# A sketched attention with a Fourier mix on one core: k alone in strided columns, last v tokens loaded apart, spare matmuls in a gap, and a new timetable of grouped matmuls

## The chip, the cores and the metric

One core of one Trainium2 chip. The metric is the time of one execution on the device in microseconds. Each kernel was run several times, and one execution was taken with the profiler. The profiled span runs from the first to the last instruction and is shorter than the time: in the runs told here by 1.8 to 2.5 us in nearly all of them, and by up to 3.4 us in a few.

With one core, a run counts as slow when it is over 1.5% above the fastest of the same kernel, and as fast otherwise. Ratios between kernels use fast runs alone, run on the same chip in the same rounds.

The engines are named as in the profile: PE is TensorE's matmuls and PEld its weight loads, DVE is VectorE, ACT is ScalarE, POOL is GpSimd, SP issues most transfers.

## The reference

Four batches of four heads, 1088 tokens, head size 32. The attention maps q and k to 64 products of two 8-wide projections each, and needs no softmax. Its output, 128 wide, goes through a Fourier transform over tokens and channels, of which the real part is kept, a normalization, and a two-layer filter. It is shown cut to what matters.

```python
def phi(x):                                   # x: (4, 4, 1088, 32)
    a = einsum('rd,bhsd->bhsr', S1, x)        # r = 8
    b = einsum('rd,bhsd->bhsr', S2, x)
    return einsum('bhsi,bhsj->bhsij', a, b).reshape(..., 64)
q_p, k_p = phi(q), phi(k)
kv = einsum('bhsf,bhsd->bhfd', k_p, v)
z = sum(k_p, axis=2)
x = einsum('bhsf,bhfd->bhsd', q_p, kv) / (einsum('bhsf,bhf->bhs', q_p, z)[..., None] + 1e-6)
x = x.transpose(0, 2, 1, 3).reshape(4, 1088, 128)
u = x + real(fft(fft(x, axis=1), axis=2))
un = (u - mean(u)) / sqrt(var(u) + 1e-6)
out = u + relu(un @ w_ch1) @ w_ch2            # (4, 1088, 128) float32
```

## The kernel before

The kernel first only notes its operations, each with one or more engines that could do it. Three lists then decide everything: `_SEQ` is the order in which the operations are issued, `_PICK` the engine of each, `_BANK` the PSUM bank of each product. Each engine works its own instructions in that order.

```python
def order(self, table):
    seq, picks, slots = table
    for o, x in zip(self.ops, picks):
        o.pick = x
    for bk, x in zip(self.banks, slots):
        bk.slot = x
    return [self.ops[n] for n in seq]
# ...
pe([(0.05, 0.2)] * WARM, e, ["dumw"], [bw], key=("prep", 0, "warm"), writes=["warm"], t=-15)  # 21 matmuls on zeros
```

A batch goes through this chain: load k, q and v; transpose k and q in blocks of 32x32 on DVE; project k, multiply the two halves (`kp`); k-times-v on PE, which needs v in `vx`; copy the result to `kvz`; project q in two large products, one of which is copied to `bsb`, mostly by ScalarE; multiply (`qp`); qp-times-kv; divide to the attention output `xb`. The mix of the batch follows: sums `yf` and `fo`, the transform (`zt`, `us`), the normalization, the two layers (`hT`), and the result `ob`, which is stored.

Buffers come in two sets, so batch 2's loads wait for batch 0's use. Loads stand in one queue in order. k and q are both transposed into strided columns:

```python
for i in range(3):                                                  # k: step of 4 fp32
    d = [[1, 2], [128, 8], [4, 32]]
    eng.transpose(_v(kT(s), 0, 128, 2 * i, d), kin(s)[:, 512 * i : 512 * i + 512])
    # ...
for i in range(3):                                                  # q: step of 8 fp32
    if STRIDED and i < 2:
        d = ([[1, 8], [256, 2], [8, 32]], [[-1, 8], [-256, 2], [8, 32]])[i]
        eng.transpose(_v(qT(s), 0, 128, o + (256 + 7) * i, d), qin(s)[:, o : o + 512])
```

v is loaded in four transfers of 288 columns; the tokens left over come in a fifth transfer that waits for those four, and the ninth and last group of k-times-v waits for it:

```python
for j in range(4):
    n = 288
    def e(q_, j=j, n=n):
        q_.dma_start(_v(vx(s), 0, 128, 640 * j, [[1, n]]), bass.AP(tensor=v.tensor, ...))
    inline(P.add(sp(128, 4 * n, e, [("vone", s)] + gate), key=("ld", b, "vx"), writes=[w], war=war, t=t))
# ...
P.add(sp(128, 128, e, [w]), aq(128, 128, e, [w]), key=("ld", b, "vr"), writes=[wr], war=war, t=t + 0.01)
# ...
pe(f32ct(64), e, [(("kp", c), b), ("vx", b), ("vone", s)] + ([("vr", b)] if c == 8 else []),
   [bkv], key=K("pkv", c), writes=[("pkv", b)], t=T + 4 + 0.5 * c, mode=1)
```

## Time and profile before

| | before |
|---|---|
| time, three runs | 90.91 us median, 90.26 to 91.88 |
| the profiled execution | 89.34 us, span 87.2 us, mean granted TensorE clock 0.98 |
| busy | PE 73.8, DVE 74.6, ACT 47.2, POOL 43.1 us |

This is PE's timeline of the kernel before, the rows that begin with a wait of over 0.3 us; columns are start and length in us, engine, line, operation, output and inputs, shapes, count, and in brackets the idle time before and what ended it:

```profile
1.22 4.44 PE L375 MATMUL bank<-dumw 128*128 128x256 bf16 x21 [1.22 <-DVE dumw L338]
8.40 1.95 PE L532 MATMUL bank<-sblk,kT 128*64 128x64 f32 x36 [2.74 <-DVE kT L500]
18.30 1.27 PE L532 MATMUL bank<-sblk,kT 128*64 128x64 f32 x36 [1.68 <-DVE kT L503]
34.47 0.27 PE L567 MATMUL bank<-vx,kp 128*64 128x64 f32 x1 [0.34 <-issue]
35.24 0.34 PE L532 MATMUL bank<-sblk,kT 128*64 128x64 f32 x4 [0.50 <-DVE kT L500]
38.85 0.23 PE L795 MATMUL bank<-cd,zt 128*128 128x128 bf16 x1 [0.45 <-ACT zt L281]
69.82 0.42 PE L753 MATMUL bank<-tab,fo 128*128 128x288 bf16 x2 [0.36 <-DVE fo L739]
```

The k projections (L532) of batches 0, 1 and 3 wait for k's transposition, in the head for 2.74 us. The same 36 matmuls take 1.95 us in the head and 1.27 us for batch 1: after the first gap the clock is halved.

### The profile page before, as it was taken

What the parts mean: (1) busy time and instruction counts of PE and PEld (TensorE: products, weight loads), DVE (VectorE), ACT (ScalarE), POOL (GpSimd) and SP (SyncE); (2) the same over time, 40 slices, a digit from 0 to 9 for tenths busy, and PEclk for the clock granted to TensorE, in tenths of its full rate; (3) what the DMA queues carried; (4) which work ended last, traced back from release to release, by engine and by line L of the source; (5) the groups of instructions that cost most, each with busy time, mean ns of one, the idle gap of its engine ahead of it and who ended that gap; (6) DMA issues with size and microseconds to landing.
All of it is one profiled execution on the core that took longest, in us unless ns stands there. A gap on an engine that the chain in (4) does not pass through costs nothing.

```text
span 87.2 us, 3358 instructions
## 1 busy us (share of the span) xinstructions
PE 73.8 (85%) x1348; PEld 55.2 (63%) x1351; DVE 74.6 (86%) x237; ACT 47.2 (54%) x129; POOL 43.1 (49%) x83
## 2 busy tenths in 40 slices
PE   4951999669999997879999999999899889998600
PEld 3731944554599956758896765796388656875500
DVE  1156979999999968999989999997999999999940
ACT  3500335015332227197999998724613999999300
POOL 7830398009949899489723220002992684620000
PEclk9999579999999999999999999999999999999999
DMA  0799999895006988000000000017260000002653
GB/s 0 167 288 346 391 368 355 315 417 224 1 8 169 297 326 271 19 8 4 8 0 0 0 23 0 0 25 209 64 213 0 4 0 8 0 0 68 190 147 106
DMA packets 8150, 10.98 MB, mean 126 GB/s; under 512 B 1608, under 2 KB 6728, under 8 KB 8136
## 3 DMA queue, kind: packets, MB, share of 16 engines
q1 hardware_dynamic: 6774, 9.80, 34.3%
q10 hardware_dynamic: 1362, 0.98, 4.0%
q8 instruction: 10, 0.16, 0.7%
q14 instruction: 4, 0.03, 0.1%
HBM read 8.55 MB, written 2.23 MB: 124 GB/s over the span
## 4 chain that ended last, share of the span: by engine, by line
PE 43%; DVE 33%; DMA 11%; ACT 3%; SPq 2%; issue 2%; DVEq 0%; ACTq 0%
DMA kin<-in_k_dram 11%; DVE qp L669 8%; PE bank L913 7%; PE bank L626 7%; DVE ob L933 6%; DVE kT L500 6%; PE bank L875 6%; PE bank L532 5%; PE bank L567 4%; DVE qT L519 3%; PE bank L795 3%; PE bank L753 3%; PE bank L692 3%; DVE xb L710 3%; PE bank L638 2%
## 5 line engine op out<-in xcount | busy, mean ns | idle before, releaser
L550 POOL TENSOR_TENSOR kp<-ab 128x256 f32<-128x256 f32 x23 | 13.7, 625 | 9.8 <-ACT ab L281 9.7
L883 ACT ACTIVATE hT<-bank 128x512 bf16<-128x512 f32 x25 | 13.6, 608 | 1.0 <-PE bank L875 1.0
L669 DVE TENSOR_TENSOR qp<-bank,bsb 128x512 f32<-128x512 f32 (+1 forms) x24 | 12.0, 541 | 0.5 <-ACT bsb L281 0.5
L567 PEld LDWEIGHTS bank<-vx,kp 128*64 128x64 f32 x288 | 9.9, 138 | 3.8 <-POOL kp L550 1.6
L729 POOL TENSOR_TENSOR yf<-xb 128x512 f32<-128x512 bf16 x6 | 6.9, 1157 | 10.6 <-DVE xb L710 10.6
L913 PE MATMUL bank<-w2b,hT 128*128 128x128 bf16 x144 | 11.9, 220 | 0.3 <-ACT hT L883 0.3
L567 PE MATMUL bank<-vx,kp 128*64 128x64 f32 x288 | 11.4, 224 | 0.3 <-issue 0.3
L739 POOL TENSOR_TENSOR fo<-yf 128x256 bf16<-128x256 f32 x15 | 11.1, 760 | 1.0 <-DVE yf L729 0.7
L913 PEld LDWEIGHTS <-hT 128*128 128x128 bf16 x144 | 9.0, 98 | 3.8 <-issue 1.0
L281 ACT COPY bsb<-bank 128x512 f32<-128x512 f32 (+1 forms) x21 | 8.2, 462 | 5.8 <-PE bank L626 5.0
L532 PE MATMUL bank<-sblk,kT 128*64 128x64 f32 x144 | 7.0, 242 | 5.1 <-DVE kT L500 3.2
L692 PE MATMUL bank<-kvz,qp 128*64 128x66 f32 x288 | 11.0, 225 | 0.3 <-DVE qp L669 0.3
L933 DVE SCALAR_TENSOR_TENSOR ob<-bank,rs,us 128x128 f32<-128x128 f32 (+1 forms) x36 | 10.2, 331 | 0.8 <-PE bank L913 0.7
L692 PEld LDWEIGHTS bank<-kvz,qp 128*64 128x64 f32 x288 | 10.0, 137 | 1.2 <-DVE qp L669 0.8
L281 ACT COPY ab<-bank 128x256 f32<-128x256 f32 (+1 forms) x7 | 2.8, 395 | 12.7 <-PE bank L532 10.1
L532 PEld LDWEIGHTS bank<-sblk,kT 128*64 128x64 f32 x144 | 5.9, 153 | 5.9 <-DVE kT L500 3.7
L875 PE MATMUL bank<-uT,w1c 128*128 128x512 bf16 x29 | 9.4, 379 | 0.2
L500 DVE STREAM_TRANSPOSE kT<-kin 128x512 f32<-128x512 f32 x8 | 8.2, 1090 | 1.2 <-DMA kin<-in_k_dram 1.2
L830 DVE BATCH_NORM_STATS2 st<-bank 128x6 f32<-128x128 f32 (+1 forms) x36 | 8.6, 272 | 0.2 <-PE bank L806 0.2
L519 DVE STREAM_TRANSPOSE qT<-qin 128x512 f32<-128x512 f32 x8 | 8.5, 1096 | 0.0
L281 ACT CAST zt<-bank 128x288 bf16<-128x288 f32 x16 | 6.1, 411 | 4.2 <-PE bank L753 4.1
L283 POOL CAST ub<-us 128x512 bf16<-128x512 f32 (+1 forms) x9 | 4.5, 506 | 5.8 <-ACT us L281 4.3
(82 smaller groups left out, 148.7 us busy)
## 6 DMA issues: line engine op xcount, KB each, us to landing
vx<-in_v_dram SPq DMA_DIRECT2D x16, 144.0 KB, 4.9
qin<-in_q_dram SPq DMA_DIRECT2D x4, 544.0 KB, 5.6
kin<-in_k_dram SPq DMA_DIRECT2D x3, 544.0 KB, 5.0
out_dram<-ob SPq DMA_DIRECT2D x9, 128.0 KB, 2.6
out_dram<-ob ACTq DMA_DIRECT2D x7, 128.0 KB, 2.4
tab<-tab_d SPq DMA_DIRECT2D x1, 864.0 KB
kin<-in_k_dram SPq DMA_DIRECT2D x1, 288.0 KB
kin<-in_k_dram SPq DMA_DIRECT2D x1, 256.0 KB, 3.2
```

Of the source, the lines that this page charges most:

```text
L281: SE.copy(o, i)
L500: eng.transpose(_v(kT(s), 0, 128, (2 if STRIDED else 64) * i, d), kin(s)[:, 512 * i : 512 * i + 512])
L519: eng.transpose(_v(qT(s), 0, 128, o + (256 + 7) * i, d), qin(s)[:, o : o + 512])
L532: PE.matmul(_v(bt(bks[bi]), 64 * th, 64, 64 * ci, [[1, 64]]), kT(s)[:, 128 * c + 64 * th : 128 * c + 64 * th + 64], sblk[:, :], start=True ...
L550: eng.tensor_tensor(out=_v(kp(s, c), 0, 128, 0, [[64, NH], [8, 8], [1, 8]]), in0=_v(bt(bks[i]) if eng is VE else ab(s, i), 0, 128, 64 * ci ...
L567: PE.matmul(_v(bt(bkv), 64 * hh, 64, 128 * p + 64 * hh, [[1, 64]]), _v(kp(s, c), 0, n, 128 * p + 64 * hh, [[1, 64]]), _v(vx(s), 0, 128, 32 ...
L669: P.add(dve(nd, lambda e, p=p, i=i, nd=nd, dd=dd, bA=bA, ah=ah: e.tensor_tensor(out=qp(s, p, i)[:, 256 * ah : 256 * ah + nd], in0=_v(bt(bA ...
L692: PE.matmul(_v(bt(bk), 64 * th, 64, 132 * ti + 66 * p, [[1, 66]]), lh, kvz(s, i & 1)[:, p, :], start=(ti == 0 and p == 0), stop=True, skip ...
L875: pe(bfmm(512), lambda m=m, c=c, bh=bh: PE.matmul(bt(bh)[:, :], w1c[:, 128 * c : 128 * c + 128], uT(s, m)[:, :], start=True, stop=True), [ ...
L883: SE.activation(out=hT(s, m)[:, c, :], in_=bt(bh)[:, :], func=ACT.Relu)
L913: PE.matmul(bt(bo)[:, 128 * i : 128 * i + 128], lh, w2b[:, c, :], start=(c == 0 and not norm), stop=(c == 3), skip_group_check=True)
L933: P.add(dve(128, lambda e, m=m, i=i, nt=nt, bo=bo: e.scalar_tensor_tensor(out=_v(ob(s, m // 2), 0, nt, at(m, i), [[1, 128]]), in0=_v(bt(bo ...
```

## The change

Its intent: take work off DVE by writing q in natural order; start k-times-v without the late tail of v; keep the TensorE clock up in the head; and issue everything in a new order, with fewer and larger schedulable pieces on PE. The diff is cut; the three lists are new throughout and are not shown.

```diff
-STRIDED = True
+WARM2 = 8
 _SEQ, _PICK, _BANK          # all three replaced
@@ tables: only the output order (kbase) is turned; a permutation stands in for the identity
-        jj, pp = jj.T, pp.T
-    kbase = [(34 * pp + 2 * jj + (2 if m == 0 else 1)).reshape(-1) for m in range(2)]
+    kbase = [(34 * pp + 2 * jj + (2 if m == 0 else 1)).T.reshape(-1) for m in range(2)]
-    cd = np.concatenate([c, -s, s, np.eye(128), np.eye(128)[::-1]], axis=1)
+    turn = (base[0][:, None] == kbase[1][None, :]).astype(np.float64)
+    cd = np.concatenate([c, -s, s, turn, turn[:, ::-1], np.eye(128)], axis=1)
@@ spare matmuls, eight times three
+        for i in range(WARM2):
+            def e(bw=bw):
+                for _ in range(3):
+                    PE.matmul(bt(bw)[:, 0:256], dumw[:, 0:128], dumw[:, 0:256], start=True, stop=True)
@@ v: 256 columns in the main loads, the rest in two loads that wait for nothing but the buffer
-            n = 288 if STRIDED or j < 3 else 320
+                vx(s)[:, j, 0:256],
...
-            P.add(sp(128, 128, e, [w]), aq(128, 128, e, [w]), key=("ld", b, "vr"), writes=[wr],
+        for j in range(2):
...
+            rd = [("vzero", s)] + gate
+            P.add(sp(128, 256, e, rd), aq(128, 256, e, rd), key=("ld", b, "vr"), writes=[w],
@@ q transposed in order
-                if STRIDED and i < 2:
-                    d = ([[1, 8], [256, 2], [8, 32]], [[-1, 8], [-256, 2], [8, 32]])[i]
-                    eng.transpose(_v(qT(s), 0, 128, o + (256 + 7) * i, d), qin(s)[:, o : o + 512])
+                eng.transpose(_v(qT(s), 0, 128, o, d),
+                              _v(qin(s), 0, 128, o, [[1, 512]] if i < 2 else d))
@@ groups: one piece for all matmuls of a column group (k-times-v shown; the others alike)
-            for p in range(2):
-                def e(c=c, p=p, n=n):
+            def e(c=c):
+                for p in range(2):
...
@@ the residual add of tile i waits for tile i's four matmuls, not for all sixteen
-                        [("po", b, m), wrs, (("us", m), b)], [bo], us=0.26), key=K("ob", m, i),
+                        [("po", b, m, i), wrs, (("us", m), b)], [bo], us=0.26), key=K("ob", m, i),
```

## The prediction

> **What bounds the kernel now.** I read the page's busy shares first, then the slices, the groups by shape, the timeline of VectorE (DVE), the DMA queue's waits, and last the chain of work that ended last.
>
> The page's first two parts, one row per engine:
>
> ```profile
> PE 73.8 (85%) x1348; PEld 55.2 (63%) x1351; DVE 74.6 (86%) x237; ACT 47.2 (54%) x129; POOL 43.1 (49%) x83
> ...
> DVE  1156979999999968999989999997999999999940
> ...
> PEclk9999579999999999999999999999999999999999
> ```
>
> No engine is full, but DVE and PE are both at 85%. One slice is 2.18 us. Slices 4 and 5 of the clock row (8.7 to 13 us) read 5 and 7: TensorE was at half rate there.
>
> The chain of work, one line by engine:
>
> ```profile
> PE 43%; DVE 33%; DMA 11%; ACT 3%; SPq 2%; issue 2%; DVEq 0%; ACTq 0%
> ```
>
> It alternates between PE and DVE, so relief of one alone is worth only part of what it saves. In order of time it holds this stretch:
>
> ```profile
> 25.24 1.03 DVE qT L519
> ...
> 26.79 1.03 DVE qT L519
> 27.83 5.26 DMA kin<-in_k_dram
> 33.12 2.07 DVE kT L500 x2
> ```
>
> Batch 3's k arrives only at 33.1 us. The queue's waits give the reason:
>
> ```profile
> SPq L463 <- PE bank L532: 4.8, 1, 4.8
> ```
>
> The v load of batch 2 stood in the in-order queue until 24.83 us, because batch 0's k-times-v matmuls still read the buffer; k of batch 3 was behind it.
>
> DVE's groups by shape, with the mean of one in ns:
>
> ```profile
> L669 DVE TENSOR_TENSOR qp<-bank,bsb 128x512 f32<-128x512 f32 x16 | 10.0, 676 | 0.0
> L519 DVE STREAM_TRANSPOSE qT<-qin 128x512 f32<-128x512 f32 x8 | 8.5, 1096 | 0.0
> L500 DVE STREAM_TRANSPOSE kT<-kin 128x512 f32<-128x512 f32 x8 | 8.2, 1090 | 1.2 <-DMA kin<-in_k_dram 1.2
> L669 DVE TENSOR_TENSOR qp<-bank,bsb 128x128 f32<-128x128 f32 x8 | 2.1, 269 | 0.5 <-ACT bsb L281 0.5
> L503 DVE STREAM_TRANSPOSE kT<-kin 128x64 f32<-128x64 f32 x4 | 1.1, 278 | 0.7 <-DMA kin<-in_k_dram 0.7
> L521 DVE STREAM_TRANSPOSE qT<-qin 128x64 f32<-128x64 f32 x4 | 0.9, 214 | 0.2 <-DMA qin<-in_q_dram 0.2
> ```
>
> The transposes of 512 columns cost 1.1 us, an arithmetic instruction of the same size 0.68 us.
>
> Milestones, from DVE's timeline: the attention output xb of batches 0 to 3 is complete at 30.5, 37.2, 60.4 and 67.4 us. The last DVE instruction ends at 83.8 us, and the last store takes the 3.4 us to 87.2.
>
> **What the Trainium skill says.** "SBUF — State Buffer", section "Door 1: The DMA port swizzle", says that SBUF has 16-byte lines and that an access which goes to a new line each time pays for it, so that a stride of up to 4 fp32 is what is free. k is written here at a step of 16 bytes, q at 32 bytes. The trace agrees: k's strided write costs (1090 - 278)/448 = 1.8 ns a column, the product qp, written in order, (676 - 269)/384 = 1.06. "Vector Engine (DVE) Microarchitecture Reference", section 3.8, says the transpose itself sustains one element per cycle per lane, so the excess should be the write and vanish with the stride. No 512-column transpose of the before kernel writes in order, so that is not yet shown.
>
> "TensorE: Matmul & The Clock Gate", section "What's actually happening", says the clock is halved after an idle window of about 3.4 us and restored after a busy one. The trace agrees: PE does nothing from 5.7 to 8.4 us, the clock is 0.50 from 8.7 to 12.1 us and 1.00 after. The warm-up matmuls themselves run at 4.44/21 = 0.21 us each; the same page's section "Back-to-back issue gap" has 0.11 us for 256 columns when warm.
>
> "DMA: Bandwidth & Descriptors", section "Specifications", wants 512 B pieces for line rate. The change turns one 128-byte-piece load per batch into two, 16 KB more in small pieces of a batch that moves over 1.6 MB; nothing to count.
>
> **The change part by part.** I had the order of the instructions of both kernels on each engine.
>
> Spare matmuls: 24 in the gap after the warm-up. At 0.11 us they fill 2.6 us, 5.7 to 8.3, and the first k matmul starts at 8.4 anyway. They keep the clock. Pace of the head before and of batch 1 at full clock: k projection 1.95 against 1.27 us, small q 0.64 against 0.39, the first half of the large q 1.69 against 1.04. Sum saved on PE: 0.68 + 0.25 + 0.65 = 1.6 us; the fp32 weight product that is put before the large q gives about 0.5 back, and DVE then waits less than it would; some 0.6 to 1 us at batch 0's last qp (16.25 before, 15.3 by my walk).
>
> q in natural order: a 512-column transpose written in order should take 214 + 448 x 1.06 = 0.69 us. 8 x (1.096 - 0.69) = 3.3 us off DVE. The order is put right by a permutation in place of the identity in matmuls that exist already: no cost. The matmuls now read q in runs of 16 fp32 in place of 512 or 8; the trace has 0.59 us for both of those, so I expect no cost.
>
> Other choices of engine, counted from the orders with the before kernel's durations, in DVE us as they follow one another (about 0.07 less than the duration): kp products 13 to 8, -1.7; relu 7 to 4, -1.8; evictions us 4 to 1, -1.4; uT 5 to 2, -0.9; bsb, ab, kvz, ea, eb together -0.7; yf 2 to 1, -0.7; against them zt 0 to 4, +1.5; fo 1 to 2, +0.9. Sum -4.8. DVE: 74.6 - 3.3 - 4.8 = 66.5. ScalarE gains 3.7 (51), GpSimd 5 products of 0.6 and one yf less some casts, 3 (46). Neither is near its span.
>
> v: the main loads carry 256 in place of 288 columns and the tail loads no longer wait for them (a 2.2 us wait of the queue before). The larger effect is the order: batch 0's k-times-v matmuls are now one run before batch 1's work, done at about 15.4 us, so the v load of batch 2 goes at 17 and k of batch 3 at about 20, landing near 26 in place of 33.
>
> Groups: the number of real matmuls is the same; residual adds may start after 4 matmuls of the last product, not 16. The last four adds can overlap it, about 0.8 us off the end.
>
> The walk, taking DVE's new order with those paces, and PE's at its own: k projection 0.035 us each, k-times-v 0.031, qp-times-kv 0.034, large q 0.065, last product 0.06, first layer 0.22, DFT 0.12. xb of batch 0 is complete at 20.3 us (before 30.5), of batch 1 at 34.4 (37.2), because in between DVE works on batches 2 and 3. Then GpSimd holds: its 15 products for batches 2 and 3 end at 37.7 us, so batch 3's k-times-v is done at 39 (before 44.5). DVE has 23 us of work to batch 3's xb (57.5 if it never waits), but I find it waiting about 1 us for the second DFT and 1.5 for the large q of batch 3: xb 2 at 52, xb 3 at 60. After that DVE has 16.3 us, the before kernel had 16.4: 76.3, with 1 to 2 us of waits 77.8; last store 3.4: span 81.2. A hand walk is optimistic, as every wait of a semaphore and every collision it misses adds; I allow 1 us: 82.
>
> **The rivals.** First, PE is the bound. From the paces its real work is about 65 us (9.0 k-times-v, 9.2 + 0.9 qp-times-kv with the added ones, 5.1, 8.3 and 1.6 projections, 8.5 and 7.5 the layers, 15 the mixing). Of these about 41 remain at batch 1's xb; from 34.4 that is 75.8, plus 3.5 us of small waits as the before kernel had in the same stretch, plus 4.2 for last add and store: 83.5. Second, the end is bound by latency: two mixes with eviction, transposition, relu and add in turn. ScalarE has about 16 us of evictions after xb 3, DVE 16. Then the earlier gains are lost in the tail, and only 2 us of the span are left as gain: 85. For it speaks that the chain shares of PE and DVE are 43 and 33%; against it that the before kernel's DVE ran that stretch nearly without a gap. Third, the spare matmuls start at half clock: 24 x 0.21 = 5 us, to 10.7, delaying the first real matmul by 2.3. Against it: the window 1.9 to 5.3 was busy and the next rate change fits 5.3. If the window falls later, half of it, 1 us. Fourth, GpSimd's in-order queue holds yf of batch 1 behind the products for longer than I walked; 1 to 2 us.
>
> **Range and chances.** Of 82 (walk), 83.5 (PE) and 85 (tail) I take 82.5 as the span. The before kernel's runs have 90.91 for a span of 87.2 in the profiled run, so 82.5/87.2 x 90.91 = 86.0 us. The runs of before spread by 1.6 us, and a walk errs by some 2 us: 83.2 to 89.2. Faster by over 2% means under 89.1; even the tail rival, 85/87.2 x 90.91 = 88.6, gives that. Faster 0.88, within 2% 0.10, slower 0.02.
>
> **What would show it.** Right: q's transposes near 0.69 us; DVE busy near 66 us; clock 1.0 in slices 4 and 5; xb at about 20, 34, 52, 60 us; no 5 us wait for k of batch 3. Wrong: q's transposes at 1.0 us (the read, not the write, was slow); spare matmuls of 0.2 us that reach past 9 us; xb 3 before 61 us and yet an end after 84, which is the tail; or PE without a gap from 35 us on, which is the PE bound. The whole is wrong if DVE is relieved and the milestones do not move.

## The result and the profile after

The changed kernel is right and takes 84.03 us in the median of four runs (83.66 to 84.76), the kernel before beside it 90.97 us (90.26 to 91.88, four runs). The ratio of the fast runs is 0.927, 95% interval 0.918 to 0.936. A ratio here is the mean time of one kernel's fast runs over the mean of the other's fast runs of the same rounds, so it is not quite the ratio of the medians. The profiled execution took 84.07 us, its span is 82.1 us.

The busy row, DVE's and the clock's slices, and the chain by engine, of the kernel after:

```profile
PE 73.7 (90%) x1375; PEld 56.7 (69%) x1375; DVE 67.0 (82%) x227; ACT 49.4 (60%) x135; POOL 45.5 (55%) x89
...
PEclk9999999999999999999999999999999999999996
...
PE 54%; ACT 16%; DMA 11%; POOL 8%; DVE 3%; issue 2%; DVEq 0%; ACTq 0%; POOLq 0%
```

DVE's work fell by 7.6 us. PE's busy time did not change (73.8 and 73.7 us) while the span fell by 5.1 us; so TensorE's idle time fell by as much, from 13.4 to 8.4 us. In the chain DVE went from 33% to 3%, and PE from 43% to 54%. The clock row has no half-rate stretch in the head.

DVE's transposes of 512 columns in the kernel after, groups by shape (busy us, mean ns of one, idle before):

```profile
L488 DVE STREAM_TRANSPOSE kT<-kin 128x512 f32<-128x512 f32 x8 | 8.5, 1105 | 1.3 <-DMA kin<-in_k_dram 1.3
...
L501 DVE STREAM_TRANSPOSE qT<-qin 128x512 f32<-128x512 f32 x8 | 5.5, 682 | 0.3 <-DMA qin<-in_q_dram 0.3
```

q's take 682 ns in place of 1096; k's, still strided, stay.

PE's timeline of the kernel after, the head and all waits of over 0.2 us that followed it:

```profile
5.55 2.78 PE L377 MATMUL bank<-dumw 128*128 128x256 bf16 x24
8.27 1.27 PE L512 MATMUL bank<-sblk,kT 128*64 128x64 f32 x36
...
13.84 2.20 PE L548 MATMUL bank<-vx,kp 128*64 128x64 f32 x66 [0.58 <-DMA vx<-in_v_dram]
16.63 1.62 PE L668 MATMUL bank<-kvz,qp 128*64 128x66 f32 x48 [0.59 <-ACT kvz L269]
21.85 0.38 PE L760 MATMUL bank<-xb,cd 128*128 128x256 bf16 x2 [0.23 <-DVE xb L685]
43.09 0.41 PE L728 MATMUL bank<-tab,fo 128*128 128x288 bf16 x2 [0.25 <-ACT hT L860]
```

All of the waits for k after the head are gone. The 24 spare matmuls fill the gap of 2.74 us, k's projection runs at its full pace of 1.27 us, and the waits that are left in the timeline sum to 1.65 us after the start, where the kernel before had 6.8 by the same count. That is about the whole of the 5.1 us by which the span shrank.

The load of batch 3's k in the queue's timeline, first of the kernel before, then of the kernel after, and DVE's timeline of the kernel after, the lines that answer to batch 3's late k:

```profile
27.83 0.54 SPq L445 DMA_DIRECT2D kin<-in_k_dram  x1
```

```profile
23.28 0.54 SPq L448 DMA_DIRECT2D kin<-in_k_dram  x1
```

```profile
29.16 1.11 DVE L488 STREAM_TRANSPOSE kT<-kin 128x512 f32<-128x512 f32 x1 [0.66 <-DMA kin<-in_k_dram]
...
76.83 1.34 DVE L909 SCALAR_TENSOR_TENSOR ob<-bank,rs,us 128x128 f32<-128x128 f32 x5
```

The wait of 4.8 us for a busy v buffer is gone. Batch 2's v loads start at 18.71 us in place of 24.83, the longest wait among them is 1.3 us, and the load of batch 3's k is issued 4.6 us earlier; the queue's one long wait for a v buffer, 2.1 us, now comes after it. Batch 3's k is transposed from 29.2 us on in place of 33.1, after a wait of 0.66 us. DVE's last work ends at 78.2 us in place of 83.8.

Reading the kernel before again with this in hand showed why its queue stood so long. The main v loads of batch 0 had to land before the small tail load was issued, at 13.62 us; the ninth group of batch 0's k-times-v waited for that, and came only at about 24.6 us, because other work stood before it in PE's order. It held the v buffer, so batch 2's v load went at 24.83 us and batch 3's k after it.

### The profile page after: what moved, and what is told of

It reads as the page before. It is cut to its first block, busy times and chain, and to the rows that moved or that the text cites. A ratio compares the mean times of both kernels' runs of the same rounds, so it can differ in the third digit from the quotient of the medians.

```text
span 82.1 us, 3421 instructions
## 1 busy us (share of the span) xinstructions
PE 73.7 (90%) x1375; PEld 56.7 (69%) x1375; DVE 67.0 (82%) x227; ACT 49.4 (60%) x135; POOL 45.5 (55%) x89
## 4 chain that ended last, share of the span: by engine, by line
PE 54%; ACT 16%; DMA 11%; POOL 8%; DVE 3%; issue 2%; DVEq 0%; ACTq 0%; POOLq 0%
PE bank L668 12%; DMA vx<-in_v_dram 11%; PE bank L548 7%; PE bank L604 6%; PE bank L728 6%; ACT hT L860 6%; PE bank L890 5%; PE bank L852 4%; PE bank L772 4%; POOL kp L532 4%; PE bank L512 3%; DVE ob L909 2%; ACT kvz L269 2%; ACT bsb L269 2%; POOL vx L345 2%
## 5 line engine op out<-in xcount | busy, mean ns | idle before, releaser
L532 POOL TENSOR_TENSOR kp<-ab 128x256 f32<-128x256 f32 x28 | 16.6, 628 | 4.9 <-ACT ab L269 4.9
L860 ACT ACTIVATE hT<-bank 128x512 bf16<-128x512 f32 x28 | 16.0, 613 | 0.5 <-PE bank L852 0.5
L704 POOL TENSOR_TENSOR yf<-xb 128x512 f32<-128x512 bf16 x7 | 8.1, 1159 | 5.2 <-DVE rs L822 5.2
L890 PE MATMUL bank<-w2b,hT 128*128 128x128 bf16 x144 | 10.8, 219 | 0.1
L548 PE MATMUL bank<-vx,kp 128*64 128x64 f32 x288 | 10.1, 224 | 0.7 <-DMA vx<-in_v_dram 0.6
L728 PE MATMUL bank<-tab,fo 128*128 128x288 bf16 x32 | 6.5, 286 | 0.2 <-ACT hT L860 0.2
L685 DVE TENSOR_TENSOR xb<-bank,rec 128x384 bf16<-128x384 f32 x12 | 6.5, 553 | 0.3
L269 ACT CAST zt<-bank 128x288 bf16<-128x288 f32 x12 | 4.7, 412 | 3.2 <-PE bank L728 3.1
L501 DVE STREAM_TRANSPOSE qT<-qin 128x512 f32<-128x512 f32 (+1 forms) x12 | 6.1, 523 | 0.3 <-DMA qin<-in_q_dram 0.3
L269 ACT COPY kvz<-bank 64x66 f32<-64x66 f32 x14 | 2.9, 210 | 5.5 <-issue 2.9
```

The costliest lines, as they stand in the source:

```text
L269: SE.copy(o, i)
L532: eng.tensor_tensor(out=_v(kp(s, c), 0, 128, 0, [[64, NH], [8, 8], [1, 8]]), in0=_v(bt(bks[i]) if eng is VE else ab(s, i), 0, 128, 64 * ci ...
L548: PE.matmul(_v(bt(bkv), 64 * hh, 64, 128 * p + 64 * hh, [[1, 64]]), _v(kp(s, c), 0, 128, 128 * p + 64 * hh, [[1, 64]]), _v(vx(s), 0, 128, ...
L728: PE.matmul(bt(bk)[:, 0:288], lh, tab[:, kpar, 3 * cs + m, :], start=(m == 0), stop=(m == 2))
L860: SE.activation(out=hT(s, m)[:, c, :], in_=bt(bh)[:, :], func=ACT.Relu)
L890: PE.matmul(bt(bo)[:, 128 * i : 128 * i + 128], lh, w2b[:, c, :], start=(c == 0 and not norm), stop=(c == 3), skip_group_check=True)
```

## The experiments

Twelve kernels, all right in their results, in three calls. The kernels of one call ran on one chip together with the kernel before; its fast runs had a mean of 90.8, 91.4 and 89.8 us in the three calls, so kernels of different calls are compared by their ratios. Only 4 of 11, 3 of 5 and 2 of 11 runs of the kernel before were fast in the three calls, so the ratios of call 3 rest on two runs of it; within call 3 the comparison with "after again" is the firmer one.

| run | fast runs, mean us | ratio to before | 95% |
|---|---|---|---|
| the change, first result | 84.1 (4 runs) | 0.927 | 0.918 to 0.936 |
| call 1: after, no spare matmuls | 84.7 (3) | 0.934 | 0.921 to 0.946 |
| call 1: after, q strided again | 84.6 (6) | 0.932 | 0.923 to 0.942 |
| call 1: before, q natural | 89.2 (2) | 0.983 | 0.965 to 1.000 |
| call 1: before, spare matmuls | 91.2 (4) | 1.006 | 0.993 to 1.018 |
| call 2: before, v tail early | 89.8 (6) | 0.982 | 0.973 to 0.990 |
| call 2: before, those three | 88.0 (3) | 0.962 | 0.946 to 0.977 |
| call 2: before, 40 more spare matmuls | 93.4 (3) | 1.020 | 1.002 to 1.039 |
| call 2: after, 40 more spare matmuls | 89.2 (6) | 0.975 | 0.967 to 0.983 |
| call 3: after again | 83.5 (4) | 0.928 | 0.919 to 0.937 |
| call 3: after, q strided and no spare | 84.8 (4) | 0.944 | 0.933 to 0.955 |
| call 3: after, v first, filter later | 84.1 (5) | 0.936 | 0.929 to 0.944 |
| call 3: after, v first | 86.1 (4) | 0.959 | 0.949 to 0.968 |

My theory was that no single part pays for the gain: the milestones move because the order lets batch 0 finish early and batch 3's k come early, and the parts that relieve DVE help little once DVE is not the bound. The rival was that DVE's relief of 7.6 us, about 3 of it from q's transposes, is what pays.

**After, without the spare matmuls.**

```diff
-                for _ in range(3):
-                    PE.matmul(bt(bw)[:, 0:256], dumw[:, 0:128], dumw[:, 0:256], start=True, stop=True)
+                pass
```

> The changed kernel without its 24 spare matmuls. Mine: TensorE idles from 5.7 to about 8.3 us, the clock falls to half for one window of 3.4 us, the k projection takes 1.9 instead of 1.27 us, and batch 0's k-times-v starts 0.6 us later than 13.8 (the large q then ends at about 14.4), so 0.5 to 1.0 us slower than the changed kernel. Rival (the head waits for v anyway, which lands at 13.8 us): 0 to 0.3 us slower.

Measured: 84.7 us, ratio 0.934, and the fast runs' spans are 82.3 to 83.3 us in place of 81.7 to 82.3. PE's timeline of its profiled (slow) execution shows what the spare matmuls prevent:

```profile
7.71 2.19 PE L511 MATMUL bank<-sblk,kT 128*64 128x64 f32 x36 [1.85 <-DVE kT L487]
9.83 0.49 PE L615 MATMUL bank<-qT,eb 32*64 32x64 f32 x8
...
14.87 2.32 PE L547 MATMUL bank<-vx,kp 128*64 128x64 f32 x72
```

The projection takes 2.19 us in place of 1.27, and k-times-v starts at 14.87 us in place of 13.84. The page's clock row shows full rate there all the same, so it is the durations that tell. Some 1 us is lost in the head of this trace, and 0.6 us of the time in the mean; by the intervals alone the 0.7% is not resolved.

**After, with q in strided columns again.** Tables, transposes, and the matmul reads of q and qp go back to the old order; nothing else changes.

```diff
-                eng.transpose(_v(qT(s), 0, 128, o, d),
-                              _v(qin(s), 0, 128, o, [[1, 512]] if i < 2 else d))
+                if i < 2:
+                    d = ([[1, 8], [256, 2], [8, 32]], [[-1, 8], [-256, 2], [8, 32]])[i]
+                    eng.transpose(_v(qT(s), 0, 128, o + (256 + 7) * i, d), qin(s)[:, o : o + 512])
```

> The changed kernel with q transposed in strided columns as before (its tables and slices put back, the order of instructions kept). VectorE gets 8 x 0.41 = 3.3 us more. If VectorE's work is on the path, 2 to 3.3 us slower than the changed kernel; rival (TensorE is the bound after the change, VectorE has gaps): 0.3 to 1.3 us slower.

Measured: 84.6 us, ratio 0.932. The transposes are back at their old price, 1094 ns, which costs DVE 3.1 us in this group:

```profile
L504 DVE STREAM_TRANSPOSE qT<-qin 128x512 f32<-128x512 f32 x8 | 8.6, 1094 | 0.5 <-DMA qin<-in_q_dram 0.5
```

The time moves by 0.5%, within the intervals, and the spans of its six fast runs, 80.8 to 83.1 us, lie on both sides of the changed kernel's 81.7 to 82.3. In the new order, DVE's relief by q is worth nothing that these runs resolve. That speaks against the rival, for q's part of the relief.

**Before, with q in natural order.** The same part alone, put into the kernel before.

```diff
-                if STRIDED and i < 2:
+                if False:
-                for vo, lh in ((0, ID), (2, JD)):
+                for vo, lh in ((0, TD), (2, JD)):
```

> The kernel before with q transposed in natural order and the permutation in the tables, nothing else. VectorE loses 3.3 us. Mine: 1 to 2 us faster than before, since 33 per cent of the chain was VectorE. Rival (the wait for batch 3's k and the order of the instructions decide): under 0.7 us faster.

Measured: ratio 0.983, interval 0.965 to 1.000, from two fast runs only. The transposes take 675 ns, so the price is that of the write, whatever the order of the rest. About 1.6 us of 91 is gained from 3.3 us taken off DVE, so about half of it; the interval allows 0 to 3.2 us, so the gain is at the edge of what is resolved.

**Before, with 24 spare matmuls.**

```diff
-WARM = 21
+WARM = 45
```

> The kernel before with 45 warm-up matmuls in place of 21 (24 more, one after the other). Mine: the clock stays at full speed, batch 0's last qp ends about 1 to 1.5 us earlier than 16.25, and the time is 0.5 to 1.3 us shorter. Rival (the extra ones run at half clock and end after 9 us): no gain or up to 1 us slower.

Measured: ratio 1.006, no gain. PE's timeline of this run:

```profile
8.52 1.27 PE L532 MATMUL bank<-sblk,kT 128*64 128x64 f32 x36
...
12.18 1.54 PE L626 MATMUL bank<-qT,eb 32*64 32x512 f32 x16 [1.36 <-DVE qT L519]
```

k's projection is quick, but q landed late in this execution, at about 10 us, and PE then stood for 1.36 us; the half-rate stretch came after that gap, from about 12.8 to 16.1 us. So the spare matmuls moved the slow stretch and did not take it away. In how many executions q is that late is not known; in the four traces of kernels with these same loads (before; before with q natural, with 24 spare matmuls, with 40 more) q's first transposition waits for q until 8.6 to 10.0 us.

**Before, with the tail of v loaded early.** The main loads carry 256 columns, the two tail loads wait for nothing but the buffer (its last columns are set to zero first), and the ninth group of k-times-v, with the two copies to `kvz` that follow it, is put right behind the other eight. The change to the list is written here as moves.

```diff
-            n = 288 if STRIDED or j < 3 else 320
+            n = 256
+    q = move(q, [10], after=9); q = move(q, [94, 95, 96, 97], after=87)   # in the list _SEQ
```

> The kernel before with v loaded as in the change (256 columns, both tails apart, no wait for the main loads), batch 0's tail directly behind its v, and batch 0's last two k-times-v groups and its kvz evictions moved up behind the other groups. Mine: the v load of batch 2 is no longer held to 24.8 us, batch 3's k lands near 27 instead of 33 us, the 1.2 us wait of VectorE for it goes, 1 to 2 us faster than before. Rival (the rest of the order stays, so the products are merely ready earlier): under 0.5 us.

Measured: ratio 0.982, interval 0.973 to 0.990, a gain of 1.6 us that is resolved. The early buffer did not bring k of batch 3 forward, though; DVE's timeline of this run:

```profile
33.63 2.14 DVE L503 STREAM_TRANSPOSE kT<-kin 128x512 f32<-128x512 f32 x2
```

There is no wait before it: k was there, its load had been issued at 21.4 us, but DVE's order places the transposition behind work that ends at 33.6. In the kernel before, the same transposition stood at 33.1 us with a wait of 1.19 us. The two starts can't be compared as they stand, because in this execution q came late and the half-rate stretch lasted to about 15.5 us: batch 0's k-times-v starts at 16.47 us in place of 14.53. Against its own head the transposition is 1.4 us earlier, about the wait that is gone. So an early load is worth only what the order lets it be worth: in this trace the wait, not the 6.4 us by which the load was issued earlier.

**Before, with the three parts together.** The edits of the three runs above.

> The kernel before with q in natural order, the 24 more warm-up matmuls, and the early v, all three. If the parts add: the sum of their single gains, 3 to 4.5 us faster than before. What is left to the change's 6.6 us is then its order of instructions and choice of engines. Rival (all three relieve the same stretch before 37 us): less than the sum, 1.5 to 2.5 us.

Measured: ratio 0.962. The three parts without the new timetable give 3.8%, interval 2.3 to 5.4%, about half of the 7.2 to 7.3% of the whole change. Singly they gave 1.7, -0.6 and 1.8%, in sum 3.0%, so the parts add as far as these runs resolve.

**Before and after, with 40 more spare matmuls spread over the run.** Five ahead of each large q product, meant as 8 x 5 x 0.11 us = 4.4 us of TensorE's time. The slope of the time against this load tells how far PE is the bound.

```diff
                 def e(wt=wt, nm=nm):
+                    for _ in range(5):
+                        PE.matmul(bt(bqs[nm][(0, 0)])[:, 0:256], dumw[:, 0:128], dumw[:, 0:256],
+                                  start=True, stop=True, skip_group_check=True)
```

> The kernel before with 5 more spare matmuls ahead of each of the eight large-q groups: 40 x 0.11 = 4.4 us more of TensorE work, spread over the kernel. Where TensorE is not the bound, well under half of it shows: 1 to 2.5 us slower. If it is the bound already in the kernel before, 3.5 to 4.4 us.

> The changed kernel with the same 4.4 us of spare TensorE work. If the change has made TensorE the bound (54 per cent of its chain, VectorE 3), 3 to 4.4 us slower than the changed kernel, and more than in the kernel before. Rival (the end is set by the chain of evictions and adds after the last attention output): 1 to 2.5 us, as in the kernel before.

Measured: the load is larger than meant. In PE's timeline of the changed kernel with the load, five spare matmuls hold back the product behind them by 0.64 us:

```profile
11.65 0.71 PE L600 MATMUL bank<-dumw 128*128 128x256 bf16 x5
12.29 1.11 PE L607 MATMUL bank<-qT,eb 32*64 32x512 f32 x16
```

Eight times that is 5.1 us; PE's busy time rose from 73.7 to 79.2 us, of which 0.7 us are slower spare matmuls in the head. So the load is about 5 us. The kernel before goes from 91.4 to 93.4 us, 1.9 us (0.2 to 3.5), in three fast runs; its three slow runs took 95.2 to 95.7 us. The changed kernel has 0.975 in place of 0.927 or 0.928, that is 0.048 x 91.4 = 4.4 us (3.3 to 5.5; across calls, so by the ratios). The slope goes from about 0.4 to about 0.9, each uncertain by 0.2 to 0.4. The chain of the loaded kernels, by engine, first before, then after:

```profile
PE 49%; DVE 30%; DMA 10%; issue 3%; SPq 2%; ACT 2%; DVEq 0%; ACTq 0%
```

```profile
PE 55%; ACT 15%; DMA 9%; SPq 5%; POOL 4%; issue 4%; DVE 2%; DVEq 0%; ACTq 0%; POOLq 0%
```

The reading that fits is that in the kernel before part of the added work falls into gaps in which PE waited (6.8 us), and that the changed one has next to none (1.65 us) to hide it in.

**After, once more.** No edit.

> The changed kernel once more, unaltered, so that the other three of this call stand against it on one chip. Both theories: its first result again, 0.92 to 0.935 of the kernel before in the fast state, a profiled span of 81.5 to 83.5 us.

Measured: 83.5 us, ratio 0.928, as the first time. Its profile differs in the head; k-times-v of batch 0 starts earlier and without a wait:

```profile
13.25 2.32 PE L548 MATMUL bank<-vx,kp 128*64 128x64 f32 x72
```

The span is 81.5 us in place of 82.1, and k-times-v ends 0.5 us sooner (15.57 us in place of 16.04), so the gain of the head seems to have gone through to the end whole.

**After, with q strided and no spare matmuls: the new timetable alone.** The edits of the first two runs together. The early tail of v stays, as the groups and the timetable are built on it.

> The changed kernel with the old strided q transposes and without the spare matmuls: what is left is the new order of the instructions, the new division between the engines, and the early load of the last v tokens. Theory 'the order carries most of it' (the single losses were about +0.5% for each part of the two, and do not grow together because TensorE is the bound): 0.930 to 0.945 of before, 0.5 to 1.5 us slower than the changed kernel. Rival 'VectorE relief is what pays, and one part covered for the other': 0.955 or more, over 2.5 us slower than the changed kernel.

Measured: 84.8 us, ratio 0.944, 1.3 us over the changed kernel of the same call, and no fast run of the one reaches into the range of the other (84.18 to 85.15 against 83.07 to 83.89). So q and the spare matmuls together are worth about 1.5%, and the timetable with its groups, engines and early v gives 5.6% of the 7.2%. That is what the theory said. The rival's 0.955 is the end of the interval, but its other sign, over 2.5 us more than the changed kernel, is not there. The run keeps the timetable's choices of engine, though: DVE is busy for 69.3 us in it, still 5.3 us less than before. So it shows what the timetable as a whole is worth, not the order by itself. This holds although the head of its profiled (slow) execution was at half rate from about 9.4 to 16.2 us.

**After, with batch 0's v loads first, and the filter's first product behind k-times-v.** The 0.58 us that PE waited for v in the first trace looked like something to win. In the list, the main v loads of batch 0 were put ahead of three constant loads, the weight product behind batch 0's k-times-v, and the nine groups into the order in which their k comes.

```diff
+    q = move(q, [16, 17, 15], after=11)     # jm, cd, w1f loads behind v
+    q = move(q, [61], after=93); q = move(q, [62], after=111)   # w1 product, its copy
```

> The changed kernel with the main v loads of batch 0 moved ahead of three constant loads, and the first product of the filter put behind batch 0's k-times-v, whose column groups run in the order in which their k arrives. Theory 'the wait for batch 0's v (the k-times-v matmuls begin at 13.84 us and still wait 0.58 us for v) is on the path': 0.7 to 1.4 us faster than the changed kernel of this call, and the k-times-v matmuls start by 12.8 us. Rival 'the loads only change places, q or k comes later by as much, or a later wait absorbs it': less than 0.3 us.

Measured: 84.1 us against 83.5, so no gain, if anything 0.6 us lost. PE's timeline:

```profile
5.65 3.51 PE L378 MATMUL bank<-dumw 128*128 128x256 bf16 x24
...
11.98 1.73 PE L605 MATMUL bank<-qT,ea 32*64 32x512 f32 x16 [0.37 <-DVE qp L648]
13.63 2.32 PE L549 MATMUL bank<-vx,kp 128*64 128x64 f32 x72
```

The wait for v is gone, but k-times-v starts at 13.63 us all the same. The spare matmuls took 3.51 us in place of 2.78 (3.12 in the run beside it), though the edit does not touch them. With the weight product of 1.1 us moved away PE waits 0.37 us for a bank that DVE empties, and the second large q product takes 1.73 us in place of 1.06, so the time which that product had filled is lost. A later wait absorbed it, as the rival said; my theory that this wait sets the head fell.

**After, with batch 0's v loads first.** The same without moving the weight product.

> As the run before, but the filter's first product stays where it was on TensorE, ahead of k-times-v, and waits for its later constants. Theory: part of the gain, 0.3 to 0.8 us faster than the changed kernel. Rival: no gain, or a loss, as TensorE stands at the filter product until its weights land.

Measured: 86.1 us, ratio 0.959, 2.6 us slower than the changed kernel of the same call:

```profile
11.65 1.10 PE L393 MATMUL bank<-w1f,jm 128*128 128x512 f32 x2 [1.27 <-DMA w1f<-in_moe_w_ch_dram]
```

PE works in order and stands 1.27 us for the weights; k-times-v starts at 14.58 us, 1.33 us later than in the run beside it. The delay comes out at the end at least whole: the profiled span is 1.7 us longer, and the mean span of the fast runs 2.2 us (83.7 in place of 81.5). Why it grew by more than 1.33 us is not shown; the rest of the 2.6 us by which the mean time grew lies outside the span.

## Why the prediction was right

It said 86.0 us, 83.2 to 89.2, faster; it was 84.03. By its steps:

| step | predicted | measured after (in brackets: after again) |
|---|---|---|
| q transpose of 512 columns | 0.69 us | 0.682 us |
| DVE busy | 66.5 us | 67.0 (67.4) us |
| spare matmuls end | 8.3 us | 8.3 (8.8) us |
| clock in the head | full | full |
| k-times-v of batch 0 done | 15.4 us | 16.0 (15.6) us |
| batch 3's k issued, transposed from | 20, 26 us | 23.3, 29.2 (22.0, 28.1) us |
| xb of batches 0 to 3 | 20.3, 34.4, 52, 60 us | 21.8, 36.2, 54.5, 61.8 (21.4, 35.3, 53.8, 61.1) us |
| last DVE instruction | 77.8 us | 78.2 (77.6) us |
| span | 82.5 us | 82.1 (81.5) us |
| time | 86.0 us | 84.03 (83.71) us |

- **The write, not the read, was what made q's transposes slow.** Right, and to about 2%: in six kernels the strided form took 1089 to 1098 ns, in eight the form in order 675 to 683. The prediction's reading that the trace agrees with the page on lines of 16 bytes holds in part only: k's step is just those 16 bytes, which the page has as free, and k's transposes cost as much as q's (1090 and 1096 ns).
- **The order moves the milestones.** Right, and the timetable as a whole, of which it is a part, carries most of the gain (the run with the timetable alone). The milestones came 1 to 2.5 us later than walked. 0.6 us of that is the wait for batch 0's v, which the walk missed; the second run did not have it. Another 0.59 (0.63) us PE waited for ScalarE's copy to `kvz`. Batch 3's k came 3 (2) us later than walked. The loss was made good at the end: from xb 3 to the end of the span it took 20.3 us where the walk had 21.2.
- **The rival that PE is the bound fits what was measured.** The prediction named the sign, PE without a gap. The trace has no wait of PE over 0.25 us after 22 us, and most of the added load came out. So the main walk, which followed DVE from xb 3 on, came to the right end (77.8 us against 78.2) along an engine that holds only 3% of the chain of the kernel after: to that extent its span was luck. The rival's number, 83.5 us of span, was 1.4 us too high, and parts of it cancel: xb 1 came 1.8 us later than it assumed, PE then took 40.6 us to its last matmul (76.9 us) where it had 41.4 plus 3.5 us of small waits, and the last add and store took 5.2 us, not 4.2.
- **The other rivals.** The tail's sign did not come: xb 3 was at 61.8 us, the end at 82.1. The spare matmuls were not at half rate to 10.7 us, but in three of the six traces that have them behind the new head they took 3.5 us, to about 9.2 us, which is the half of this rival, 1 us. GpSimd's products stand in the chain from 19.9 to 22.9 us, but PE had other work then; its only wait there is 0.23 us, for DVE.
- **What was mis-sized is the conversion of the span to a time.** The span of 82.5 us was 0.4 us off, the time 2 us. The prediction scaled by 90.91/87.2, that is, it put 3.7 us between span and time. But the execution with the span of 87.2 us took 89.34 us itself, 2.1 us more; 90.91 is the median of other, slower executions, whose spans, by the same difference, were near 88.8 (a run of 90.97 us had just that span). With 2.1 us added, 82.5 would have given 84.6.
- **What DVE's relief is worth.** The prediction counted on 8.1 us of it without saying what q's 3.3 us are worth alone. In the kernel before about half of them came through (interval 0 to all), in the changed one none that can be seen. The remainder of the relief, the other choices of engine, is part of the timetable, and no run takes it out: what it is worth is not shown.

What stays open: the new order, the choice of engines, the groups and the early v cannot be taken apart by an edit of a few lines, because the lists refer to the pieces by number. The runs show their sum (5.6%) and that the early v alone gives 1.8% in the old order. Adding 3.8% for the three parts and 5.6% for the order with v, and taking away the v that is in both, gives 7.6%, near the 7.2% measured; the intervals are about 1% each, so this is a check and not a decomposition.

## What to carry to other kernels

When two engines are both at 85% and change places in the chain, a new timetable of order and engines can be worth more than a cheaper instruction on either (here 5.6%, against 0.5 to 1.7% for q's transposes); look for the engine's own waits and for the operation that holds a buffer which a queue waits for. Then measure what bounds the new kernel with an extra load on one engine, whose size is read from the trace and not taken from the plan (here 5 us, not 4.4): a slope near 0.4 suggests that gaps remain to be filled, a slope near 1 that less work on that engine is what helps. And convert a span into a time with the overhead of the same execution, not with the median of others.

## What the Trainium skill lacked or had wrong

- "TensorE: Matmul & The Clock Gate", section "What's actually happening", has the clock halved after an idle window of about 3.4 us. Here it was halved after shorter gaps: 2.74 us (before), 2.04 and then 1.33 us with work between (the timetable alone), 0.58 and then 1.36 us (spare matmuls in the kernel before). The half-rate stretches then lasted 3.4, 6.8 and 3.3 us. That the window is free-running, as the section also says, fits the 24 spare matmuls behind the new head, which took 2.78 to 3.52 us in six executions; no run here shows the window itself.
- "SBUF — State Buffer", section "Door 1: The DMA port swizzle", has a stride of up to 4 fp32 as free. A DVE transposition written at just that step, k's, was not: 1.8 ns a column ((1090 - 278)/448), where q's written in order took 1.06 ns ((682 - 206)/448). At twice the step, q's in the kernel before, 512 columns took the same as k's, 1096 ns against 1090. No page gives the price of a transposition with a strided destination; the nearest, "Vector Engine (DVE) Microarchitecture Reference", section 5.2, times strided destinations of another operation.
- No page says how much the landing of the same loads differs between executions: q's first transposition, with a wait for q before it, started between 8.6 and 10.0 us in four traces that issue the same loads as the kernel before, and between 7.7 and 9.3 us in four with the loads of the kernel after. One profiled execution of the kernel before was 1.6 us faster than the median of its timed ones.
